# Attention by packed tokens and a gated feed-forward layer on one core: the beginning in one traced order, first softmaxes from PSUM by token halves, first batch in steps of four f tiles, Softplus/Erf gates in 32 units

## The chip, the core and the metric

The kernel runs on one core of a Trainium2 chip. Its engines are TensorE (PE; its weight loads are PEld), VectorE (DVE), ScalarE (ACT), GpSimd (POOL) and SyncE (SP), which issues most DMAs. Each runs its own instructions in order and waits for the others by semaphores. The metric is the device time of one execution in microseconds; several executions were timed, and one more was recorded by the profiler.

## The reference, cut to what matters

```python
# 8 batches, 8 heads, 576 tokens, head_dim 64, 32 packed tokens, d_model 512, d_ff 2048
p_packed = sm_attn(p, k, v)                  # the 32 packed tokens look at k and v
out = sm_attn(q, p_packed, p_packed)         # every token looks at the packed tokens
x = out.transpose(0, 2, 1, 3).reshape(B * S, H * D)
h = x @ w_in                                 # w_in, w_out: float64 arrays
sp = np.maximum(h, 0.0) + np.log1p(np.exp(-np.abs(h)))     # softplus
g = h * erf(sp)
return (g @ w_out).astype(np.float32)
```

## The kernel before, in words

**Units.** A batch b has 576 tokens, taken in two halves c of 288. The 2048 columns of d_ff are taken in eight steps i of 256 (two f tiles of 128). A unit is one (b, c, i); there are 128. Batches 0 and 1 come in four segments each: steps 0 to 3 of both halves of batch 0, the same of batch 1, then steps 4 to 7 of batch 0, then of batch 1. The batches 2 to 7 go through all eight steps of one half before the other. Where a batch comes in two turns, the second turn adds to the output in memory by an accumulating DMA of POOL (L318); the first writes by SP (L320).

**Work of a unit.** `h_block`: 12 matmuls (L264) give h for 256 columns, as three products of split operands: `a2h` and `a2l` are the high and low part of the second softmax (transposed), `wph` and `wpl` those of wp = p_packed times w_in. ACT copies h from PSUM into `hs` (L267). The gate h * erf(softplus(h)) is approximated by four ACT functions, Tanh, Square, Tanh, Tanh (L270, L271, L272, L275), and three DVE instructions (L273, L274 and a last multiplication, L280 or L283). `o_block`, LAG = 3 units later: the unit's share of g @ w_out (L308). For the first WHOLE = 12 units g and w_out go in as F32, 16 matmuls; after that both are split into two parts (g: L286, L287; w_out: `woh` L103 on ACT, `wol` L104 on DVE), 24 matmuls. At a segment's end ACT copies the sums out (`ob`, L315).

**Attention and wp.** `attention(b)` is a generator of 12 stages, which the main loop advances between units: first scores `s` (L165), softmax over 576 tokens (L170 to L179), transposes `t` (L186), the packed tokens `p` (L198), second scores `s` (L212), softmax over the 32 packed tokens in a transposed layout (L215 to L229), `a2h`, `a2l` (L232, L233). `w_prime(b, j)` computes one of four wp blocks of 512 columns (L243; copies L245, L246). Attention of batch 1 begins with unit 0 (ATT1).

**Weights.** w_in and w_out arrive as float64, in 32 tiles of 128 x 512 (512 KB each). `load_f32` issues the DMA into a staging tile (L83), ACT takes the high words to F32 (L87), and three DVE instructions put the bits together (L88, L89, L90). The staging pool `spool` has two places; six early loads borrow places of `wpool` (EARLY). A load into a place waits until the conversion that used it before has ended. Tile names: `wi_c` is block c of w_in on its way, `wos` a tile of w_out on its way, `wo` the converted one.

**Order.** The program is traced unit by unit, with a plan that attaches stages, loads and conversions to units; a scheduler then orders each engine's instructions by its own estimate of times. Nothing else pins the order, except one `high_priority` block.

Of the kernel before, what the change touches and what calls it, by code (L numbers as in the profile page):

```python
# [28 lines left out]
def tile_pack_attention_moe(ctx: ExitStack, tc: tile.TileContext, qT, kT, v, pT, w_in, w_out, outT):  # L29
# [23 lines left out]
    CONV = 2  # L53
# [22 lines left out]
    def load_f32(dst, src, name, pool=None, tag="wst"):  # L76

        if src.dtype == F32:
            nc.sync.dma_start(dst, src)
            return  # L80
        n = src.shape[1]
        st = (pool or spool).tile([P, n], I64, name=name, tag=tag)
        nc.sync.dma_start(st[:], src)  # L83
# [3 lines left out]
        nc.scalar.activation(dst, high.bitcast(F32), AF.Abs, scale=F64_SCALE)  # L87
        nc.vector.tensor_scalar(bits, bits, 3, None, op0=ALU.logical_shift_left)  # L88
        nc.vector.scalar_tensor_tensor(bits, high, 0x80000000, bits, op0=ALU.bitwise_and, op1=ALU.bitwise_or)  # L89
        nc.vector.scalar_tensor_tensor(bits, low, 29, bits, op0=ALU.logical_shift_right, op1=ALU.bitwise_or)  # L90

    def load_w_in(j, c, **slot):
        load_f32(w_in_sb[:, c, j * FB:(j + 1) * FB], w_in[c * P:(c + 1) * P, j * FB:(j + 1) * FB], f"wi{j}_{c}", **slot)

    def load_w_out(f, **slot):
        made = opool.tile([P, DM], F32, name=f"wo{f}", tag="wo")
        load_f32(made[:], w_out[f * P:(f + 1) * P, :], f"wos{f}", **slot)
        wo[f] = made

    def split_w_out(f):  # L100
# [4 lines left out]
        wo_hi[f], wo_lo[f] = hi, lo  # L105

# [7 lines left out]
    def attention(b, roomy=False):  # L114
# [45 lines left out]
        a1 = apool.tile([P, 2, S], F32, name=f"a1_{b}", tag="big")  # L160
        for c2 in range(2):
# [8 lines left out]
        nc.vector.tensor_reduce(m[:], a1[:], axis=AX.X, op=ALU.max)  # L170
        nc.vector.tensor_scalar(m[:], m[:], -SCALE, None, op0=ALU.mult)
        sm = apool.tile([P, 2], F32, name=f"sm{b}", tag="sm")
        for r in range(2):
            nc.scalar.activation(a1[:, r, :], a1[:, r, :], AF.Exp, bias=m[:, r:r + 1], scale=SCALE,
                                 accum_out=sm[:, r:r + 1])
# [7 lines left out]
        for j in range(NT):  # L183
            for r in range(2):
                o = (j % 2 * 2 + r) * P
                nc.tensor.transpose(banks[0][j // 2][:, o:o + P], a1[:, r, j * P:(j + 1) * P], ident[:])  # L186
        copy_out(a1t[:, 0:NT].rearrange("p (x j) r k -> p x (j r k)", x=2), banks, 512)
# [5 lines left out]
        nc.scalar.copy(a1t[0:REM, NT].rearrange("p r k -> p (r k)"), pr[0:REM, 0:2 * P])  # L193
        for j in range(NCH):
# [8 lines left out]
        nc.vector.tensor_copy(ptt[:], po[:, 0:P])  # L203
        pt[b] = ptt
        yield
        nb = HT // 32
        ta = apool.tile([P, 2, S], F32, name=f"ta{b}", tag="big")
        for c2 in range(2):
# [5 lines left out]
            for r in range(2):  # L214
                nc.vector.transpose(ta[:, r, c2 * HT:(c2 + 1) * HT], banks[0][r][:, 0:HT])  # L215
            yield
        blocks = ta[:].rearrange("p r (n k) -> p (r n) k", k=NK)
        mx = apool.tile([P, 4 * nb], F32, name=f"mx{b}", tag="mx")
        wide = mx[:].unsqueeze(2).to_broadcast([P, 4 * nb, NK])
        nc.vector.tensor_reduce(mx[:], blocks, axis=AX.X, op=ALU.max)  # L220
        nc.vector.tensor_tensor(blocks, blocks, wide, op=ALU.subtract)
        nc.scalar.activation(ta[:], ta[:], AF.Exp, scale=SCALE)
        yield
        nc.vector.tensor_reduce(mx[:], blocks, axis=AX.X, op=ALU.add)
        nc.vector.tensor_scalar(mx[:], mx[:], 1e-9, None, op0=ALU.add)
        nc.vector.reciprocal(mx[:], mx[:])
        nc.vector.tensor_tensor(blocks, blocks, wide, op=ALU.mult)
        tb = apool.tile([P, 2, S], F32, name=f"tb{b}", tag="big")
        nc.vector.transpose(tb[:].rearrange("p r s -> p (r s)"), ta[:].rearrange("p r s -> p (r s)"))  # L229
        hi = apool.tile([P, 2, S], F32R, name=f"a2h{b}", tag="a2h")  # L230
        lo = apool.tile([P, 2, S], F32R, name=f"a2l{b}", tag="a2l")
        nc.scalar.copy(hi[:], tb[:])  # L232
        nc.vector.tensor_tensor(lo[:], tb[:], hi[:], op=ALU.subtract)  # L233
        a2[b] = (hi, lo)
        yield

    def w_prime(b, j):
        hi = wpool.tile([P, 2, FB], F32R, name=f"wph{b}_{j}", tag="wph")
# [7 lines left out]
        nc.vector.tensor_tensor(lo[:], ps[:], hi[:], op=ALU.subtract)  # L246
        wp[b, j] = (hi, lo)

    gs = {}

    def h_block(b, c, i, whole):


        hs = tpool.tile([P, 2, HT], F32, name=f"hs{b}_{c}_{i}", tag="hs")
        for k in range(2):
# [4 lines left out]
            n = 0  # L260
            ahi, alo = a2[b]
            for r in range(2):
                for w, a in ((whi, ahi), (whi, alo), (wlo, ahi)):
                    nc.tensor.matmul(ps[:, 0:HT], w[:, r, fo:fo + P], a[:, r, c * HT:(c + 1) * HT],  # L264
                                     start=(n == 0), stop=(n == 5))
                    n += 1
            nc.scalar.mul(hs[:, k, :], ps[:, 0:HT], 0.5)  # L267
# [8 lines left out]
        if whole:  # L276
            k = len(wholes) % 2
            wholes.append(i)
            g = tpool.tile([P, 2, HT], F32, name=f"g{b}_{c}_{i}", tag=("gh", "gl")[k], bufs=2)
            nc.vector.scalar_tensor_tensor(g[:], t[:], 1.0, hs[:], op0=ALU.add, op1=ALU.mult)  # L280
            gs[b, c, i] = (g,)
            return
        nc.vector.scalar_tensor_tensor(hs[:], t[:], 1.0, hs[:], op0=ALU.add, op1=ALU.mult)  # L283
        ghi = tpool.tile([P, 2, HT], F32R, name=f"gh{b}_{c}_{i}", tag="gh", bufs=2)
        glo = tpool.tile([P, 2, HT], F32R, name=f"gl{b}_{c}_{i}", tag="gl", bufs=2)
        nc.vector.tensor_copy(ghi[:], hs[:])  # L286
        nc.vector.tensor_tensor(glo[:], hs[:], ghi[:], op=ALU.subtract)  # L287
        gs[b, c, i] = (ghi, glo)
# [35 lines left out]
    segs = [(b, c, i0, i1) for i0, i1 in zip(TURNS, TURNS[1:]) for b in range(NB0) for c in range(2)]  # L324
# [15 lines left out]
    plan = {}  # L340
    conv = {}
    for i in range(NBLK):
        ph = max(n for n, start in enumerate(TURNS) if i >= start)
        items = []
        if i % 2 == 0:
            items += [("wi", i // 2, c) for c in range(4)]
        items += [("wo", 2 * i), ("wo", 2 * i + 1)]
        conv.setdefault(ph, []).append(items)
    for ph, lists in conv.items():
        if ph == 0:  # L350
            for k, items in enumerate(lists):
                for it in items:
                    at(WI_AT[k // 2] if it[0] == "wi" else k + 1).append(it)
        else:
            flat = [it for items in lists for it in items]
            n0, n1 = (2 * NB0 * TURNS[p] for p in (ph - 1, ph))
            for k, it in enumerate(flat):
                at(n0 + CONV + k * (n1 - n0 - 2 * CONV) // len(flat)).append(it)
# [18 lines left out]
    for k, (b, j) in enumerate(uses):  # L377
        if b not in ready:
# [8 lines left out]
    for f in range(DFF // P):  # L387
        made = max(n for n, its in plan.items() if ("wo", f) in its)
# [84 lines left out]
```

## Time and profile before

| what | value |
|---|---|
| executions timed | 793.75, 792.89, 793.60 us, median 793.6 us |
| profiled execution | 789.89 us, its span 788.1 us, mean granted clock 0.968 |
| PE busy | 744.6 us, 94% of the span |
| DVE busy, ACT busy | 599.7 us (76%), 597.6 us (76%) |
| POOL busy | 15.1 us (2%) |
| read from memory, written | 45.61 MB, 11.80 MB |

The profiled execution is 3.7 us shorter than the median of the timed ones; times of single pieces are from it. In the lines of the profile, L12 is line 12 of the kernel printed above, `out<-in` names the tiles that are written and read, `xN` counts instructions, and a bracket at a line's end gives the engine's idle time ahead of it and what ended it.

### The profile page before, as it was taken

To read this page: it belongs to the slowest core of one execution; us is meant where nothing else is said; L and a number is where in the kernel's file an instruction comes from. 1 tells how busy PE (TensorE), PEld (TensorE's weight loads), DVE (VectorE), ACT (ScalarE), POOL (GpSimd) and SP (SyncE) were. 2 spreads that over 40 slices of the span, in tenths; PEclk is the share of its full clock that TensorE was granted. 3 is DMA by queue.
4 is the path that set the end of the run, shared out by engine and by line. 5 is a ranking of instruction groups with operands and counts; after the bars stand their busy time and mean duration, and the time that the engine had idled before them with its cause. 6 is when DMAs were issued, how large, how long until landed. Compare 5 with 4: busy or idle time off the path is not lost.

```text
span 788.1 us, 15219 instructions
## 1 busy us (share of the span) xinstructions
PE 744.6 (94%) x6256; PEld 664.1 (84%) x6256; DVE 599.7 (76%) x916; ACT 597.6 (76%) x1011; POOL 15.1 (2%) x22
## 2 busy tenths in 40 slices
PE   3549988999999999999999999999999999999998
PEld 2228756899998898899799998889888998899998
DVE  3887898977689678867887769767886769766664
ACT  3357778988689878887687868778687867878784
POOL 0000000000111100000000000000000000000000
PEclk8568999999999999999999999999999999999999
DMA  8834735002542422013200222002300210000000
GB/s 306 291 110 149 243 116 162 31 17 67 107 88 31 83 76 89 1 39 98 80 32 1 83 81 72 13 1 80 132 32 1 79 47 1 31 2 31 1 31 31
DMA packets 31813, 58.39 MB, mean 74 GB/s; under 512 B 3584, under 2 KB 14848, under 8 KB 31744
## 3 DMA queue, kind: packets, MB, share of 16 engines
q1 hardware_dynamic: 29440, 55.06, 21.5%
q0 software_dynamic: 2304, 2.36, 2.6%
q8 instruction: 49, 0.80, 0.4%
q14 instruction: 20, 0.16, 0.1%
HBM read 45.61 MB, written 11.80 MB: 73 GB/s over the span
## 4 chain that ended last, share of the span: by engine, by line
PE 82%; DVE 7%; DMA 6%; ACT 3%; issue 1%; SPq 0%; ACTq 0%
PE o L308 50%; PE h L264 24%; PE wp L243 4%; DMA wi<-w_in 4%; DMA wos<-w_out 2%; PE p L198 2%; PE s L212 1%; PE s L165 1%; PE t L186 1%; DVE w_in_sb L89 1%; ACT t L270 1%; DVE wo L89 1%; ACT wo L87 1%; DVE w_in_sb L90 1%; DVE g L280 0%
## 5 line engine op out<-in xcount | busy, mean ns | idle before, releaser
L308 PE MATMUL o<-gl,woh 128*128 128x288 f32 x928 | 273.3, 295 | 0.0
L308 PE MATMUL o<-gh,woh 128*128 128x288 f32 x928 | 273.1, 300 | 0.0
L308 PE MATMUL o<-gh,wol 128*128 128x288 f32 x928 | 272.9, 295 | 0.0
L308 PEld LDWEIGHTS o<-gh,woh 128*128 128x128 f32 x928 | 172.1, 187 | 25.5 <-DVE t L273 8.9
L308 PEld LDWEIGHTS o<-gl,woh 128*128 128x128 f32 x928 | 174.3, 188 | 1.8 <-issue 1.3
L308 PEld LDWEIGHTS o<-gh,wol 128*128 128x128 f32 x928 | 174.6, 188 | 1.5 <-issue 1.3
L267 ACT ACTIVATE hs<-h 128x288 f32<-128x288 f32 x256 | 103.2, 412 | 95.4 <-PE h L264 94.6
L264 PE MATMUL h<-a2h,wph 128*128 128x288 f32 x512 | 155.2, 304 | 10.6 <-ACT wph L245 5.9
L264 PE MATMUL h<-a2l,wph 128*128 128x288 f32 x512 | 152.7, 298 | 1.8 <-DVE a2l L233 1.8
L264 PE MATMUL h<-a2h,wpl 128*128 128x288 f32 x512 | 152.6, 298 | 0.0
L283 DVE SCALAR_TENSOR_TENSOR hs<-t,hs 128x576 f32<-128x576 f32 x116 | 87.7, 756 | 72.5 <-ACT t L275 72.5
L275 ACT ACTIVATE t<-t,bias 128x576 f32<-128x576 f32 x128 | 98.8, 772 | 25.3 <-DVE t L274 25.0
L264 PEld LDWEIGHTS h<-a2h,wph 128*128 128x128 f32 x512 | 97.2, 190 | 22.3 <-ACT wph L245 6.8
L273 DVE SCALAR_TENSOR_TENSOR t<-t,hs 128x576 f32<-128x576 f32 x128 | 95.9, 750 | 20.1 <-ACT u L272 19.8
L270 ACT ACTIVATE t<-hs,bias 128x576 f32<-128x576 f32 x128 | 99.6, 778 | 2.9
L271 ACT ACTIVATE t<-t,bias 128x576 f32<-128x576 f32 x128 | 99.3, 775 | 2.3
L264 PEld LDWEIGHTS h<-a2l,wph 128*128 128x128 f32 x512 | 97.4, 190 | 4.3 <-DVE a2l L233 2.8
L272 ACT ACTIVATE u<-t,bias 128x576 f32<-128x576 f32 x128 | 99.3, 776 | 1.8
L264 PEld LDWEIGHTS h<-a2h,wpl 128*128 128x128 f32 x512 | 97.3, 190 | 1.9 <-issue 1.9
L274 DVE SCALAR_TENSOR_TENSOR t<-u,t 128x576 f32<-128x576 f32 x128 | 96.3, 752 | 1.6
L287 DVE TENSOR_TENSOR gl<-hs,gh 128x576 fp32r<-128x576 f32 x116 | 87.3, 753 | 1.5
L286 DVE CAST gh<-hs 128x576 fp32r<-128x576 f32 x116 | 52.9, 456 | 35.0 <-PE o L308 33.8
(60 smaller groups left out, 637.3 us busy)
## 6 DMA issues: line engine op xcount, KB each, us to landing
k<-kT SPq DMA_DIRECT2D x32, 288.0 KB, 4.3
q<-qT SPq DMA_DIRECT2D x32, 288.0 KB, 4.3
outT<-ob SPq DMA_DIRECT2D x64, 144.0 KB, 1.8
wi<-w_in SPq DMA_DIRECT2D x16, 512.0 KB, 6.0
v<-v SPq DMA_DIRECT2D x32, 256.0 KB, 3.6
wos<-w_out SPq DMA_DIRECT2D x16, 512.0 KB, 3.6
outT<-ob POOLq DMA_DIRECT2D x16, 144.0 KB, 3.7
v<-v SPq DMA_DIRECT2D x8, 128.0 KB, 4.2
```

The source lines that it names most:

```text
L264: nc.tensor.matmul(ps[:, 0:HT], w[:, r, fo:fo + P], a[:, r, c * HT:(c + 1) * HT], start=(n == 0), stop=(n == 5))
L267: nc.scalar.mul(hs[:, k, :], ps[:, 0:HT], 0.5)
L270: nc.scalar.activation(t[:], hs[:], AF.Tanh, bias=bias[:, 0:1], scale=2.0 * T_SCALE)
L271: nc.scalar.activation(t[:], t[:], AF.Square, bias=bias[:, 1:2], scale=Q_SCALE)
L272: nc.scalar.activation(u[:], t[:], AF.Tanh, bias=bias[:, 2:3], scale=U_SCALE)
L273: nc.vector.scalar_tensor_tensor(t[:], t[:], 0.5 * A2, hs[:], op0=ALU.mult, op1=ALU.add)
L274: nc.vector.scalar_tensor_tensor(t[:], u[:], 0.5 * A1, t[:], op0=ALU.mult, op1=ALU.add)
L275: nc.scalar.activation(t[:], t[:], AF.Tanh, bias=bias[:, 3:4], scale=2.0 * A_SCALE)
L283: nc.vector.scalar_tensor_tensor(hs[:], t[:], 1.0, hs[:], op0=ALU.add, op1=ALU.mult)
L286: nc.vector.tensor_copy(ghi[:], hs[:])
L287: nc.vector.tensor_tensor(glo[:], hs[:], ghi[:], op=ALU.subtract)
L308: nc.tensor.matmul(acc[b, c][d][:, 0:HT], w[f][:, d * P:(d + 1) * P], gg[:, k, :], start=(first and k == 0 and n == 0), stop=(last and k = ...
```

## The change

- **Gates.** In the first 32 units (GROUPED) the gate is Softplus, Erf (ACT) and one multiplication (DVE). The gates come in 13 groups (ENDS gives the last unit of each): all Softplus of a group, then all Erf, each kind behind an `ACT_TABLE_LOAD`; `in_turn` fixes the order of these functions on ACT. In these units o blocks follow five units behind (LAG_G) and not three, and `hs` alternates between two tags by groups. From unit 32 on the gate is the one of before.
- **Segments.** Batch 0's steps 0 to 3 come as two turns (0 to 1 and 2 to 3, each for both halves), so there are ten segments in batches 0 and 1, with eight more output tiles of 128 x 288 copied by ACT and added by POOL than before.
- **Whole units.** WHOLE goes from 12 to 8. w_out is split from unit 7 on (SPLIT) and not from 14.
- **Beginning.** The first stages, loads, conversions and two units are written out by hand, and `keep_order` ties each instruction of PE, DVE, ACT and SP there to the one before it in the traced order. 33 dummy matmuls (`keep_busy`: 6, 10, 3, 14) on the identity stand among them.
- **First attention.** For batch 0 (`roomy`) the scores stay in PSUM: maxima and exponentials read them there, by halves of 288 tokens, and the second softmax goes by two halves (`Tokens`, near and far).
- **Plan.** Attention of batch 1 is attached to units 1 to 5, not 0 to 2; the conversions are attached by FIRST and LATER. The cast of a conversion is a multiplication by 2^-112, not Abs with that scale.

```diff
@@ constants @@
+    GROUPED = 4 * NBLK
+    LAG_G = 5
...
-    TURNS = (0, NBLK // 2, NBLK)
-    WHOLE = 12
-    SPLIT = 14
-    WI_AT = (-1, 1)
-    ATT1 = (0, 2)
+    HB = NBLK // 2
+    WHOLE = 2 * HB
+    SPLIT = 7
+    ATT1 = (1, 5)
...
+    FIRST = {0: [("wo", 2), ("wo", 3)], 1: [("wi", 1, c) for c in range(4)],
+             3: [("wo", 4), ("wo", 5)], 4: [("wo", 6), ("wo", 7)]}
+    LATER = (5, 14)
+    ENDS = (1, 3, 5, 7, 10, 13, 15, 18, 21, 24, 27, 29, 31)
@@ attention @@
-            copy_out(a1[:, :, c2 * HT:(c2 + 1) * HT], banks, HT)
+            if roomy:
+                scores.append(banks[0])
+            else:
+                copy_out(a1[:, :, c2 * HT:(c2 + 1) * HT], banks, HT)
...
+        near, far = Tokens(0, HT), Tokens(HT, S)
+        for c2, half in enumerate((near, far)):
+            for r in range(2):
+                nc.vector.transpose(ta[:, r, half.cols], scores[2 + c2][r][:, 0:HT])
+            if half is near:
+                near.max()
+                near.exp()
+        yield
+        near.sum()
+        near.turn()
+        near.high()
...
@@ gates @@
+    def gate_group():
+
+        ts = []
+        for hs, b, c, i, whole in group:
+            t = tpool.tile([P, 2, HT], F32, name=f"t{b}_{c}_{i}", tag="t0")
+            in_turn(nc.scalar.activation(t[:], hs[:], AF.Softplus))
+            ts.append(t)
+        for t in ts:
+            in_turn(nc.scalar.activation(t[:], t[:], AF.Erf))
+        for t, (hs, b, c, i, whole) in zip(ts, group):
+            if whole:
+                nc.vector.tensor_tensor(whole_g(b, c, i)[:], t[:], hs[:], op=ALU.mult)
+            else:
+                nc.vector.tensor_tensor(hs[:], t[:], hs[:], op=ALU.mult)
+                split_g(hs, b, c, i)
+        group.clear()
@@ segments @@
-    segs = [(b, c, i0, i1) for i0, i1 in zip(TURNS, TURNS[1:]) for b in range(NB0) for c in range(2)]
+    turns = [(0, 0, HB // 2), (0, HB // 2, HB), (1, 0, HB), (0, HB, NBLK), (1, HB, NBLK)]
+    segs = [(b, c, i0, i1) for b, i0, i1 in turns for c in range(2)]
@@ beginning @@
+    def keep_busy(n):
+
+        for _ in range(n):
+            nc.tensor.matmul(idle[:, 0:P], ident[:], ident[:], start=True, stop=True)
+
+    start = len(traced)
     first = attention(0, roomy=True)
...
+    (b4, e4), (b5, e5) = fetch("wo", 0), fetch("wo", 1)
+    keep_busy(6)
...
+    h_block(*units[1][:3], True, 1)
+    end = len(traced)
...
+        while behind <= n - (LAG_G if n < GROUPED else LAG):
+            o_block(*units[behind])
+            behind += 1
+    keep_order(start, end)
```

In the rows of the order the batch number is left out of a name: in `o_1_0_3`, `h_0_0_0` or `hs_0_1` the first digit is the half c, the second the step i, a third the column tile; the last number is a running one.

First, ACT ahead of the first gates of batch 1 (`t_0_0` is the gate of its first unit). Before:

```order
L270 ACTIVATE t_0_0_936<-hs_0_0_919,bias 128x576
L271 ACTIVATE t_0_0_936<-t_0_0_936,bias 128x576
L272 ACTIVATE u_0_0_937<-t_0_0_936,bias 128x576
L87 ACTIVATE wo_1100<-wos_1101 128x512
L267 ACTIVATE hs_0_1_966<-h_0_1_0_967 128x288
L267 ACTIVATE hs_0_1_966<-h_0_1_1_975 128x288
L245 CAST wph_3_1040<-wp_3_1042 128x1024
L270 ACTIVATE t_0_1_983<-hs_0_1_966,bias 128x576
L267 ACTIVATE hs_0_2_1007<-h_0_2_0_1008 128x288
L275 ACTIVATE t_0_0_936<-t_0_0_936,bias 128x576
```

After, ahead of the same unit's Erf, in the group of its first three units:

```order
L404 COPY hs_0_1_969<-h_0_1_0_970 128x288
L115 CAST woh_1187<-wo_1176 128x512
L404 COPY hs_0_1_969<-h_0_1_1_978 128x288
L94 ACTIVATE wo_1252<-wos_1253 128x512
L404 COPY hs_0_2_1012<-h_0_2_0_1013 128x288
L374 ACTIVATE t_0_1_1031<-hs_0_1_969 128x576
L404 COPY hs_0_2_1012<-h_0_2_1_1021 128x288
L374 ACTIVATE t_0_2_1033<-hs_0_2_1012 128x576
L377 ACT_TABLE_LOAD
L377 ACTIVATE t_0_0_1029<-t_0_0_1029 128x576
L377 ACTIVATE t_0_1_1031<-t_0_1_1031 128x576
L377 ACTIVATE t_0_2_1033<-t_0_2_1033 128x576
```

Before, four functions of a unit stand by themselves, with a weight cast now and then between two of them; after, three units' functions stand behind the last cast of a weight tile (`wos_1253` is the 32nd load).

Second, PE around batch 1's first unit (`h_0_0_0`; `wp` are its wp blocks and the later ones of batch 0). Before:

```order
L308 MATMUL o_1_0_3_910<-g_1_2_836,wo_661 128x288
L243 MATMUL wp_2_784<-w_in_sb,pt_237 32x512 x8
L308 MATMUL o_1_0_0_907<-g_1_3_894,wo_713 128x288
L308 MATMUL o_1_0_0_907<-g_1_3_894,wo_720 128x288
L308 MATMUL o_1_0_1_908<-g_1_3_894,wo_713 128x288
L308 MATMUL o_1_0_1_908<-g_1_3_894,wo_720 128x288
L308 MATMUL o_1_0_2_909<-g_1_3_894,wo_713 128x288
L308 MATMUL o_1_0_2_909<-g_1_3_894,wo_720 128x288
L308 MATMUL o_1_0_3_910<-g_1_3_894,wo_713 128x288
L308 MATMUL o_1_0_3_910<-g_1_3_894,wo_720 128x288
L264 MATMUL h_0_0_0_920<-a2h_597,wph_0_601 128x288
L264 MATMUL h_0_0_1_928<-a2h_597,wph_0_601 128x288
```

After, from the instruction behind batch 0's last o block of the first turns on:

```order
L255 MATMUL s_0_1_627<-q_1_471,pt_624 32x288 x2
L255 MATMUL s_0_1_627<-q_1_472,pt_624 32x288 x2
L255 MATMUL s_0_1_627<-q_1_473,pt_624 32x288 x2
L255 MATMUL s_0_1_627<-q_1_474,pt_624 32x288 x2
L255 MATMUL s_1_1_669<-q_1_471,pt_624 32x288 x2
L255 MATMUL s_1_1_669<-q_1_472,pt_624 32x288 x2
L255 MATMUL s_1_1_669<-q_1_473,pt_624 32x288 x2
L255 MATMUL s_1_1_669<-q_1_474,pt_624 32x288 x2
L346 MATMUL wp_0_735<-w_in_sb,pt_624 32x512 x8
L346 MATMUL wp_1_748<-w_in_sb,pt_624 32x512 x8
L346 MATMUL wp_2_802<-w_in_sb,pt_269 32x512 x8
L400 MATMUL h_0_0_0_903<-a2h_681,wph_0_733 128x288
```

Before, a wp block stands between two o blocks of batch 0, and the second scores stand further ahead; after, batch 1's second scores and the wp blocks follow the last o block and precede the first h.

Third, DVE where the first block of the second quarter of w_in is finished (`wi_0`; its last instruction frees a staging place). Before:

```order
L88 TENSOR_SCALAR wo_572<-wo_572 128x512
L89 SCALAR_TENSOR_TENSOR wo_410<-wos_411,wo_410 128x512
L88 TENSOR_SCALAR w_in_sb<-w_in_sb 128x512
L89 SCALAR_TENSOR_TENSOR wo_565<-wos_566,wo_565 128x512
L88 TENSOR_SCALAR w_in_sb<-w_in_sb 128x512
L89 SCALAR_TENSOR_TENSOR wo_572<-wos_573,wo_572 128x512
L233 TENSOR_TENSOR a2l_274<-tb_271,a2h_273 128x1152
L90 SCALAR_TENSOR_TENSOR wo_410<-wos_411,wo_410 128x512
L89 SCALAR_TENSOR_TENSOR w_in_sb<-wi_0_417,w_in_sb 128x512
```

After:

```order
L380 TENSOR_TENSOR g_0_1_398<-t_0_1_392,hs_0_1_373 128x576
L97 TENSOR_SCALAR wo_400<-wo_400 128x512
L97 TENSOR_SCALAR wo_407<-wo_407 128x512
L98 SCALAR_TENSOR_TENSOR wo_400<-wos_401,wo_400 128x512
L97 TENSOR_SCALAR w_in_sb<-w_in_sb 128x512
L98 SCALAR_TENSOR_TENSOR wo_407<-wos_408,wo_407 128x512
L97 TENSOR_SCALAR w_in_sb<-w_in_sb 128x512
L99 SCALAR_TENSOR_TENSOR wo_400<-wos_401,wo_400 128x512
L98 SCALAR_TENSOR_TENSOR w_in_sb<-wi_0_414,w_in_sb 128x512
L99 SCALAR_TENSOR_TENSOR wo_407<-wos_408,wo_407 128x512
L98 SCALAR_TENSOR_TENSOR w_in_sb<-wi_1_420,w_in_sb 128x512
L99 SCALAR_TENSOR_TENSOR w_in_sb<-wi_0_414,w_in_sb 128x512
```

After, the multiplications of the first gate group stand ahead of it (the first row is the second of them), and four conversions go in turns; before, the low part of batch 0's softmax stands among four conversions.

More of the change, by code (lines that the diff above doesn't have):

```diff
@@ L221, in attention @@
[L221 to L227, printed above, removed]
+            if roomy:
+                scores.append(banks[0])
+            else:
+                for r in range(2):
+                    nc.vector.transpose(ta[:, r, c2 * HT:(c2 + 1) * HT], banks[0][r][:, 0:HT])
+                yield
@@ L235, in attention @@
+        yield
+        near.sum()
+        near.turn()
+        near.high()
+        yield
+        far.max()
+        near.low()
+        yield
+        far.exp()
+        yield
+        far.sum()
+        far.turn()
+        far.high()
+        yield
+        far.low()
         yield
```

282 lines of the change are left out of this document (192 added, 90 removed).

## The prediction

> **What bounds the kernel now.** I read the page first: busy time, slices, chain.
>
> ```profile
> span 788.1 us, 15219 instructions
> PE 744.6 (94%) x6256; PEld 664.1 (84%) x6256; DVE 599.7 (76%) x916; ACT 597.6 (76%) x1011; POOL 15.1 (2%) x22
> PE   3549988999999999999999999999999999999998
> PEclk8568999999999999999999999999999999999999
> PE 82%; DVE 7%; DMA 6%; ACT 3%; issue 1%; SPq 0%; ACTq 0%
> ```
>
> PE is the bound, except at the left end: a slice is 19.7 us, and the seven first slices hold all the gaps (but the end's) and all the reduced clock. The windows (length, then busy time of PE, PEld, DVE, ACT, POOL with instruction counts, granted clock, DMA share, GB/s) put edges on that:
>
> ```profile
> 0.00:64.00 64.00, 29.79 (x259) 18.83 (x260) 44.00 (x80) 28.69 (x48) 0.70 (x6) 0.65 0.67 229
> 64.00:140.00 76.00, 69.83 (x471) 51.09 (x470) 64.80 (x102) 58.53 (x101) 0.00 (x0) 0.96 0.51 164
> 140.00:236.00 96.00, 96.00 (x786) 88.71 (x785) 76.13 (x119) 80.73 (x145) 7.28 (x8) 1.00 0.27 63
> ```
>
> From 140 us on PE never stops. So the end of the kernel is: the time at which PE has its work without gaps, plus the PE work then left. Everything in the change is worth what it does to these two. The pieces and counts of PE (timeline and chain: start, length; groups up to 138.1 us: count, busy, mean ns) say where before stands at that time:
>
> ```profile
> 42.53 0.85 PE L264 MATMUL h<-a2h,wph 128*128 128x288 f32 x2 [4.24 <-ACT a2h L232]
> 131.84 4.04 PE L308 MATMUL o<-g,wo 128*128 128x288 f32 x16
> 138.10 6.09 PE o L308 x24
> 144.19 1.60 PE h L264 x12
> 172.72 3.19 PE o L308 x24
> L308 PE MATMUL o<-g,wo 128*128 128x288 f32 x145 | 39.6, 429 | 1.8 <-DVE g L280 1.8
> L264 PE MATMUL h<-a2h,wph 128*128 128x288 f32 x52 | 18.1, 354 | 10.6 <-ACT wph L245 5.9 <-ACT a2h L232 4.2 <-ACT hs L267 0.5
> ```
>
> An h block is 1.60 us (12 records, 4 of each kind), a split o block 3.19 (24 records), a whole one 4.04 (16). Up to 138.1 PE has done 52/4 = 13 h blocks and 145/16 = 9 whole o blocks; then the gapless part starts, with batch 1's second unit (the first ran alone at 131.84).
>
> What holds it back until then is the weights. They come as 64-bit words through two staging places, cast on ACT (L87), finished by three DVE instructions (L88 to L90); a new load waits on SP until a conversion has freed a place. SP's own loads and waits:
>
> ```profile
> 48.15 1.83 SPq L83 DMA_DIRECT2D wi<-w_in  x2
> 118.96 0.34 SPq L83 DMA_DIRECT2D wi<-w_in  x1
> 120.69 12.62 SPq L83 DMA_DIRECT2D wos<-w_out  x4
> L83 SPq DMA_DIRECT2D wos<-w_out x12: 327/328/340, 57.3 to 133.0; - x12
> L83 SPq DMA_DIRECT2D wi<-w_in x8: 327/328/632, 48.1 to 119.0; - x8
> DMA to landing us min/median/max: 3.4/3.8/6.0
> SPq L83 <- DVE wo L90: 31.3, 12, 7.9
> SPq L83 <- DVE w_in_sb L90: 30.7, 9, 7.2
> 48.15:133.00 84.85, 72.01 (x487) 52.69 (x487) 70.96 (x114) 62.89 (x107) 0.00 (x0) 0.91 0.52 167
> ```
>
> 20 of the 32 loads are such refills, from 48.15 to 133.0: 19 steps of 4.47 us. SP spends 31.3 + 30.7 us of them waiting for L90. DVE is busy in 84% of the stretch (70.96 of 84.85), so a conversion often queues there behind gates and attention. The durations that I use:
>
> ```profile
> L87 ACT ACTIVATE wo<-wos 128x512 f32<-128x512 f32 x16 | 10.6, 672 | 6.0 <-DMA wos<-w_out 6.0
> L88 DVE TENSOR_SCALAR wo<-wo 128x512 uint32<-128x512 uint32 x11 | 4.6, 422 | 2.8 <-ACT wo L87 2.7
> L89 DVE SCALAR_TENSOR_TENSOR wo<-wos,wo 128x512 uint32<-128x512 uint32 x13 | 8.9, 685 | 0.1
> L90 DVE SCALAR_TENSOR_TENSOR wo<-wos,wo 128x512 uint32<-128x512 uint32 x14 | 9.6, 684 | 0.0
> L267 ACT ACTIVATE hs<-h 128x288 f32<-128x288 f32 x256 | 103.2, 412 | 95.4 <-PE h L264 94.6
> L270 ACT ACTIVATE t<-hs,bias 128x576 f32<-128x576 f32 x128 | 99.6, 778 | 2.9
> L275 ACT ACTIVATE t<-t,bias 128x576 f32<-128x576 f32 x128 | 98.8, 772 | 25.3 <-DVE t L274 25.0
> L273 DVE SCALAR_TENSOR_TENSOR t<-t,hs 128x576 f32<-128x576 f32 x128 | 95.9, 750 | 20.1 <-ACT u L272 19.8
> L286 DVE CAST gh<-hs 128x576 fp32r<-128x576 f32 x116 | 52.9, 456 | 35.0 <-PE o L308 33.8
> L287 DVE TENSOR_TENSOR gl<-hs,gh 128x576 fp32r<-128x576 f32 x116 | 87.3, 753 | 1.5
> L104 DVE TENSOR_TENSOR wol<-wo,woh 128x512 fp32r<-128x512 f32 x6 | 4.1, 684 | 0.0
> L315 ACT COPY ob<-o 128x288 f32<-128x288 f32 x80 | 30.2, 399 | 6.8 <-PE o L308 6.8
> L71 ACT ACT_TABLE_LOAD x1 | 1.3, 1283 | 0.7 <-PEq L465 0.7
> ```
>
> **The change, part by part.**
>
> *Gates of the first 32 units.* Four ACT functions become two: 32 x 2 x 0.778 = 49.8 us less. The order has 35 table loads against 1: 34 x 1.283 = 43.6 us more. ACT is 6 us better off. DVE loses two instructions a unit: 32 x 2 x 0.75 = 48 us less. Behind 140 us none of it counts, PE being full; before, it frees DVE for conversions. Softplus and Erf are not in this trace; I take them at L270's 0.778 (same shape). At half of it ACT would gain 25 us more over 32 units, at twice it would lose 50; neither end is near, since the four functions of before lie within 6 ns of each other. The one table load of the trace took 1.283 us, on an idle ACT. The Trainium skill (ScalarE: Activation LUTs, section What ACT_TABLE_LOAD costs) puts some 1380 ns of drain on top of those 1283 for every switch to another set; by it ACT would come out 41 us worse off, not 6 better, and the sum would be about 810 instead of 800. The load agrees, the drain no row here shows.
>
> *Beginning and first softmax.* Scores are read from PSUM and the softmax goes by halves of 288 tokens, most conversions behind it. In before its passes run from 28 to 42.5 us, of this size (timeline, first and last of eight):
>
> ```profile
> 30.56 1.35 DVE L220 TENSOR_REDUCE mx<-ta 128x36 f32<-128x1152 f32 x1
> 41.33 1.15 ACT L232 CAST a2h<-tb 128x1152 fp32r<-128x1152 f32 x1 [1.42 <-DVE tb L229]
> ```
>
> Halved, and without the conversions that stand among them, they let the first h begin by my estimate at 28 to 31 us instead of 42.5. Two h blocks at half clock (6.4), two copies not hidden (0.8), two table loads (2.6) and four functions (3.1) then put the first gates' end at about 42, and batch 0's first four units need nothing but weights that are already there. This lead is real, and it is off the path: what PE does early is work that PE would otherwise have done while waiting later. The 33 dummy matmuls stand where PE waits; they cost nothing while PE has gaps there, and 33 x 0.13 (3.19/24) = 4 us, 9 at half clock, if it had none.
>
> *Refills.* This term decides. The order shows ten loads issued freely and 22 refills, against 20 before, and on DVE the first place comes free only behind the first group's two multiplications and, interleaved with three others, the ninth conversion: 42 + 0.8 + 12 x 0.6 = about 49.4. That is before's 48.15 again: the early start does not start the refills. From there 21 steps. Bounds for a step: a bare round is landing 3.8, cast 0.67, three instructions 1.79, with two places 3.1 us; the slow end is before's 4.47. For the value I scale by DVE: before has 114 instructions in this stretch, after by its order 103 (20 conversions, 13 wo splits, four wpl, batch 1's softmax, six gates of one multiplication), so 84.85 x 103/114 = 76.7 us. ACT in the same stretch gets nine table loads (11.5) and eight more output copies (3.2) and drops 12 functions of those six gates (9.3): +5.4, of which I count half, 2.7, since half of ACT's waits here lie beside a landing. Last refill: 49.4 + 76.7 + 2.7 = 128.8, a step of 3.78.
>
> *Order in front of batch 1.* In before batch 1's first gate stands behind the cast of the 29th weight tile. In after the cast of the 32nd, the last, stands on ACT ahead of the first Softplus's companions and of all Erfs of the group. So 128.8 is followed by landing 3.8, cast 0.67, two copies 0.82, two Softplus 1.56, table load 1.28, first Erf 0.78, and on DVE three multiplications, one wol, gh and gl in their order, 4.6: PE goes on at 142.3. PE cannot fill that time: its order has, between batch 0's last o and batch 1's first h, only batch 1's second scores and three wp.
>
> *Work left behind that point.* After has done 12 h blocks and 8 whole o blocks. It has 1.60 of h more to do; 4 x 3.19 of split o where before had 3 x 4.04 of whole o: 1.60 + 12.76 - 12.12 = +2.2 us. (Eight whole o blocks instead of twelve are a gain of 4 x 0.85 over the run, contained in this.)
>
> *Small things at nothing:* eight more accumulating output DMAs on POOL (busy 2%), the cast by a multiplication instead of Abs (same engine and shape), copies without the factor 0.5. Their cover is ACT's gaps; bare they are below 1 us.
>
> Sum: 142.3 - 138.1 + 2.2 = +6.4. The profiled execution took 789.9 us, so 796.3; the median of the runs shown, 793.6, lies 3.7 above it, so **800.0**. PE goes gapless at X: the result is 793.6 + X - 135.9.
>
> Clock: it was granted at 0.65 up to 64 us, with PE busy less than half of the time; the hole between batch 0's last o (about 98) and batch 1's first h can bring that back. Three h blocks and three wp at half clock cost up to 6 us more of PE, and nothing at the other end, since PE waits there for the gate; I take nothing.
>
> **The rivals.**
>
> *The round gets short (faster).* If casts and conversions always find ACT and DVE free, a step falls toward 3.1; at 3.2 the last refill goes at 116.6, X is 130.1, the result 787.8. For it: 48 us fewer DVE gate instructions, SP waiting 62 us for L90 before. Against: in after's order 13 wo splits and batch 1's softmax stand among the last ten conversions. It decides below a step of 3.48 (X = 135.9).
>
> *Nothing moves.* DVE's scaling alone without ACT's 2.7, and a tail shorter by 2: X = 137.6, the result 795.3; with refills from 47 it is 793. The start at 48 to 49 in both kernels speaks for it.
>
> *Table loads cost more than their row (slower).* If a load among gates must first let ACT run empty and so holds it twice as long, the nine in the refill stretch cost 11.5 more, half counted 5.8. Behind X, ACT has 24 gates of the new kind at 0.82 + 1.56, 22 loads and 16 output copies, 92 us; 28 more make 120, against PE's 24 x 3.19 + 20 x 1.60 + batch 2's attention of about 9 = 118, with ACT's waits for PE on top, some 4 more: 810. For it: ACT has no other long row that alternates its functions. Against it: ACT is idle for a quarter of the time, and a drain would partly lie there. The page named above has this case as its rule.
>
> **How the numbers follow.** Forecast (X 138 to 157, 796 to 815): 0.42. Shorter round: 0.30. Nothing moves: 0.14. Dear table loads (800 to 815, beside the forecast's own spread): 0.14. A measurement of this kernel tells 0.2%, 1.6 us, from no change. Faster is the short round, plus a little of nothing-moves: 0.32. Same: 0.13. Slower: 0.55. The low end is a step of 3.1 with a tail 2 us shorter, X = 126, 783; the high end before's own 4.47: last refill 143.3, X = 156.8, 814.5. Less than 2 in 10 lie outside. The likeliest case alone has 796 to 812.
>
> **What would show it.** First h near 30, first o near 43: the beginning is right. Refills from about 49 to 129 in 21 steps: the deciding term. PE idle between about 98 and 130 with the release by wo, w_in_sb or wph: the hole. ACT's cast of the last wo tile waiting for its DMA just ahead of the first group of three Erfs: the tail. Wrong I am if refills start well before 45 (a place freed early), if the step is under 3.5, if PE still has gaps behind 145 with ACT full (table loads), or if the DVE instructions overlap more than now.

## The result, and the profile after

The changed kernel takes 805.99 us in the median of four runs (805.10 to 808.86) where the kernel before takes 793.67 (792.89 to 794.35): a ratio of 1.0162, with a 95% interval of 1.0134 to 1.0189. It is slower, as forecast, but by 12.3 us and not by 6.4. The profiled execution is the longest of the four, 808.86 us; its page, to be held against the lines shown of before:

```profile
span 806.9 us, 15383 instructions
PE 751.1 (93%) x6354; PEld 670.8 (83%) x6354; DVE 565.8 (70%) x874; ACT 593.2 (74%) x993; POOL 22.7 (3%) x30
PE   7687853799999999999999999999999999999998
PEclk9879965899999999999999999999999999999999
PE 77%; ACT 8%; DMA 7%; DVE 5%; issue 2%; SPq 0%; ACTq 0%
```

The first slices of PE are fuller than before (7687 against 3549), and a new hole stands in the sixth and seventh (5 and 3), with the clock down. The windows (columns as before) put a size on it:

```profile
0.00:64.00 64.00, 48.55 (x347) 34.78 (x348) 39.09 (x78) 30.02 (x55) 0.70 (x6) 0.84 0.59 200
64.00:140.00 76.00, 45.35 (x335) 27.75 (x334) 54.86 (x89) 47.09 (x77) 7.42 (x8) 0.77 0.64 186
140.00:236.00 96.00, 90.06 (x752) 81.86 (x753) 45.96 (x75) 70.02 (x119) 3.54 (x4) 0.97 0.22 60
```

Ahead of 64 us PE is busy for 18.8 us more than before (11.6 of it the dummies), then for 24.5 less up to 140 and 5.9 less behind. What the early start gives is given back, and more. The hole's edges on PE (timeline: start, length, and in brackets the idle time ahead and what ended it):

```profile
44.56 7.20 PE L444 MATMUL o<-g,wo 128*128 128x288 f32 x16 [3.31 <-DVE g L380]
125.49 1.96 PE L346 MATMUL wp<-w_in_sb,pt 64*32 64x512 f32 x16 [6.78 <-DVE wpl L350]
137.86 0.85 PE L400 MATMUL h<-a2h,wph 128*128 128x288 f32 x2 [3.88 <-ACT a2h L298]
156.21 0.80 PE L444 MATMUL o<-gh,woh 128*128 128x288 f32 x4 [1.29 <-DVE gh L358]
158.91 0.40 PE L400 MATMUL h<-a2h,wph 128*128 128x288 f32 x1 [0.32 <-ACT hs L404]
```

What PE waits for between 100 and 140 us (in total, times, longest):

```profile
PE wp L346 <- DVE wpl L350: 11.3, 2, 6.8
PE h L400 <- ACT a2h L298: 3.9, 1, 3.9
PE s L255 <- DVE pt L246: 2.6, 1, 2.6
PE wp L346 <- DVE ta L261: 2.5, 1, 2.5
PE h L400 <- DVE a2l L301: 1.0, 1, 1.0
PE s L255 <- DVE ta L261: 1.0, 1, 1.0
```

These 22.3 us are all waits for steps of batch 1's attention and for wp blocks; none is for a converted weight or a gate.

SP's first and last refills, the landing times of the refills, and the window between the two:

```profile
50.82 0.94 SPq L88 DMA_DIRECT2D wi<-w_in  x2
132.62 11.81 SPq L88 DMA_DIRECT2D wos<-w_out  x4
DMA to landing us min/median/max: 3.4/4.3/6.0
50.82:144.10 93.28, 62.63 (x425) 39.53 (x424) 64.19 (x103) 55.89 (x95) 7.42 (x8) 0.80 0.62 183
```

The last of SP's four loads from 132.62 on goes at 144.1. From 158.9 on PE is gapless but for 1.8 us. Two things come late ahead of it. The refills: from 50.8 to 144.1, 21 steps of 4.44 us, as slow as before's 4.47 although DVE is now busy for 69% of the stretch only (64.19 of 93.28) and not 84%. And batch 1's attention: its `a2h`, without which no h of batch 1 begins, is cast at 136.7 us, in before at 114.6 (timeline of ACT, before's row first):

```profile
114.58 1.15 ACT L232 CAST a2h<-tb 128x1152 fp32r<-128x1152 f32 x1
136.67 1.14 ACT L298 CAST a2h<-tb 128x1152 fp32r<-128x1152 f32 x1
```

The two are not apart: the steps of batch 1's softmax stand on DVE between conversions. Ahead of the transpose whose result `a2h` is cast from, 27 of the 32 conversions are finished, 17 of them refills; in before it is 25 and 13. Four more refills at 4.44 us and a first refill 2.7 us later make 20.4 of the 22.1 us by which `a2h` comes later, an estimate from these counts.

### The profile page after: what moved, and what is told of

The parts are those of the page before. It is cut to its first block, busy times and chain, and to the rows that moved or that the text cites. A ratio compares the mean times of both kernels' runs of the same rounds, so it can differ in the third digit from the quotient of the medians.

```text
span 806.9 us, 15383 instructions
## 1 busy us (share of the span) xinstructions
PE 751.1 (93%) x6354; PEld 670.8 (83%) x6354; DVE 565.8 (70%) x874; ACT 593.2 (74%) x993; POOL 22.7 (3%) x30
## 4 chain that ended last, share of the span: by engine, by line
PE 77%; ACT 8%; DMA 7%; DVE 5%; issue 2%; SPq 0%; ACTq 0%
PE o L444 47%; PE h L400 22%; DMA wos<-w_out 3%; PE wp L346 3%; DMA q<-qT 2%; PE p L241 2%; DMA wi<-w_in 1%; PE s L255 1%; ACT L374 1%; ACT t L374 1%; DMA v<-v 1%; PE s L188 1%; ACT hs L404 1%; ACT L377 1%; ACT t L377 1%
## 5 line engine op out<-in xcount | busy, mean ns | idle before, releaser
L444 PE MATMUL o<-gh,woh 128*128 128x288 f32 x960 | 283.4, 300 | 1.4 <-DVE gh L358 1.3
L444 PE MATMUL o<-gl,woh 128*128 128x288 f32 x960 | 283.1, 296 | 0.0
L444 PE MATMUL o<-gh,wol 128*128 128x288 f32 x960 | 282.5, 295 | 0.0
L406 ACT ACTIVATE hs<-h 128x288 f32<-128x288 f32 x192 | 77.9, 413 | 75.8 <-PE h L400 73.1
L423 DVE SCALAR_TENSOR_TENSOR hs<-t,hs 128x576 f32<-128x576 f32 x96 | 72.6, 757 | 56.3 <-ACT t L419 56.2
L419 ACT ACTIVATE t<-t,bias 128x576 f32<-128x576 f32 x96 | 74.2, 773 | 19.3 <-DVE t L418 18.8
L417 DVE SCALAR_TENSOR_TENSOR t<-t,hs 128x576 f32<-128x576 f32 x96 | 71.9, 749 | 15.3 <-ACT u L416 15.3
L414 ACT ACTIVATE t<-hs,bias 128x576 f32<-128x576 f32 x96 | 74.6, 777 | 2.3
L416 ACT ACTIVATE u<-t,bias 128x576 f32<-128x576 f32 x96 | 74.7, 778 | 1.8
L415 ACT ACTIVATE t<-t,bias 128x576 f32<-128x576 f32 x96 | 74.1, 772 | 1.5
L418 DVE SCALAR_TENSOR_TENSOR t<-u,t 128x576 f32<-128x576 f32 x96 | 72.3, 753 | 0.8
```

The source lines that it names most:

```text
L414: nc.scalar.activation(t[:], hs[:], AF.Tanh, bias=bias[:, 0:1], scale=2.0 * T_SCALE)
L415: nc.scalar.activation(t[:], t[:], AF.Square, bias=bias[:, 1:2], scale=Q_SCALE)
L416: nc.scalar.activation(u[:], t[:], AF.Tanh, bias=bias[:, 2:3], scale=U_SCALE)
L417: nc.vector.scalar_tensor_tensor(t[:], t[:], 0.5 * A2, hs[:], op0=ALU.mult, op1=ALU.add)
L418: nc.vector.scalar_tensor_tensor(t[:], u[:], 0.5 * A1, t[:], op0=ALU.mult, op1=ALU.add)
L419: nc.scalar.activation(t[:], t[:], AF.Tanh, bias=bias[:, 3:4], scale=2.0 * A_SCALE)
```

## The experiments

All times are against runs of the kernel before on the same chip in the same session, so ratios are compared; before's median lay between 791.0 and 792.2 us in these sessions. "Changed" is the changed kernel at 1.0162. The bands of the expectations are meant beside 793.6 us for the kernel before, unless they name another time. An edit changes the scheduler's order behind it too; where that matters, the trace is read.

### Is it the staging round?

e1, a third place for the changed kernel, and e2, the same edit for the kernel before:

```diff
-    spool = ctx.enter_context(tc.tile_pool(name="stage", bufs=2))
+    spool = ctx.enter_context(tc.tile_pool(name="stage", bufs=3))
```

> The changed kernel with three staging places in place of two, nothing else (the scheduler orders anew). Theory A (the time is set by the round trip of a staging place: landing, wait for ACT, cast, wait for DVE, three instructions, 8.9 us a place, so 4.44 us a refill with two): with three a refill takes about 3 us, DVE's 64 us of work in the stretch then bound it, the last load goes near 120 instead of 144, PE is gapless from about 132 instead of 156, the kernel takes about 782. Theory B (the round is not it: batch 1's softmax and wp blocks on DVE, the table loads and PE's order in front of batch 1 set the end): loads come earlier, but the kernel stays above 800.

> The kernel before with three staging places. Theory A: the same bound stood there, 4.47 us a refill; with three places DVE's 71 us bound the stretch from 48, so the last load goes near 120 instead of 133 and the kernel takes about 782. Theory B: within 3 us of 793.6.

Measured: e1 1.0089 (1.0071 to 1.0108), 799.9 us; e2 1.0026 (1.0015 to 1.0038), 793.7 us. SP's last load and ACT's a2h, of e1 and then of e2:

```profile
116.90 0.33 SPq L88 DMA_DIRECT2D wos<-w_out  x1
130.47 1.15 ACT L298 CAST a2h<-tb 128x1152 fp32r<-128x1152 f32 x1 [1.91 <-DVE tb L292]
```

```profile
104.35 8.97 SPq L83 DMA_DIRECT2D wos<-w_out  x3
120.71 1.15 ACT L232 CAST a2h<-tb 128x1152 fp32r<-128x1152 f32 x1 [0.33 <-DVE tb L229]
```

The last load comes 27 us earlier in e1 and 20 us in e2. In e1 the kernel gains 0.7%, some 6 us, which is what a2h moves by; in e2 a2h comes 6 us later, and nothing is gained. By the traces more conversions are finished on DVE ahead of the transpose that feeds a2h, 31 of 32 instead of 27 in e1 and 30 instead of 25 in e2: earlier loads put more work in front of it. Theory A, that the round by itself sets the time, has fallen (it gave 782 for both kernels); it was also the prediction's deciding term. The round is worth 0.7% in the changed kernel.

### Is it the gates, the splits, the segments?

e3 sets `GROUPED = 0` (the old gates everywhere, and with them o blocks three units behind and no groups), e4 has `WHOLE = 12` and `SPLIT = 14`:

> The changed kernel with the four-function gates of before in all units (so no table loads among gates, three DVE instructions a gate, o blocks three units behind); beginning, segments and whole units stay as changed. Theory A: gates are not on the path that sets the end, the refill step stays at 4.3 to 4.6 us, 801 to 810. Theory C (table loads and grouping are the cost): 790 to 797. Theory D (lighter gates gave something back): above 812.

> The changed kernel with 12 whole units and the w_out splits from unit 14 on, as before. Theory A with the order: 14 to 16 splits leave the stretch ahead of batch 1's first gate (about 10 us on DVE, 9 on ACT), and the last weight cast stands behind the first group's Erf; PE is gapless 8 to 12 us earlier, 3.4 us more matmul time, so 797 to 802. Theory B' (splits lie in waits anyway): 807 to 811.

Measured: e3 1.0224 (1.0206 to 1.0241), some 811 us beside 793.6, between the bands of theories A and D and against theory C: with all else changed, the new gates with their grouping gain some 0.6%. e4 1.0127 (1.0112 to 1.0142): a third of a per cent back, short of theory A's gain; a2h stands at 130.2 there.

e7 has `LATER = (5, 20)`; e8 has batch 0's steps 0 to 3 in one turn for each half:

> The changed kernel with its last sixteen loads and conversions attached to units 5 to 20, not 5 to 14. In its order 31 casts instead of 32 stand ahead of batch 1's first Erf and 28 instead of 29 ahead of its a2h. Theory A or E: one refill step earlier, 3 to 6 us, 800 to 803. Otherwise unchanged, 804 to 808.

> The changed kernel with batch 0's steps 0 to 3 in one turn for each half, as before (eight output copies and eight accumulating output DMAs fewer). Theory E or A: the copies of ACT that wait for o blocks stand in front of some casts, but the refill round mostly waits for landings; 0 to 4 us less, 802 to 806. If the early output tiles and their DMAs hold up the refills (landing 4.3 us in the median instead of 3.8): 796 to 800.

Measured: e7 1.0132 (1.0110 to 1.0154), 0.3% less, somewhat under what was expected of one refill step, and its interval overlaps the changed kernel's; e8 1.0210 (1.0181 to 1.0239), missed: the finer turns gain about 0.5%, and eight more output tiles are no cost.

### Is it the place of batch 1's attention?

e5 takes back one number of the change, e6 adds the third place, e9 puts the changed number into the kernel before:

```diff
e5, e6
-    ATT1 = (1, 5)
+    ATT1 = (0, 2)
e9
-    ATT1 = (0, 2)
+    ATT1 = (1, 5)
```

> The changed kernel with batch 1's attention attached to units 0 to 2, as before, not 1 to 5. In its order batch 1's second scores and wp blocks stand among batch 0's o blocks again, and 28 of the 32 weight casts, not all 32, stand on ACT ahead of the first Erf of batch 1. Theory E (two chains of like length end in batch 1's first gate, the refills and batch 1's attention; the change delayed the second and put it behind the first): PE is gapless 14 to 20 us earlier, 787 to 795. Theory A (refills alone, by their step): the four refills that no longer stand ahead are worth the same 14 to 18 us, but with three places on top nothing more. Theory F (the attention only takes DVE's time from the conversions wherever it stands): 802 to 809.

> The changed kernel with batch 1's attention at units 0 to 2 and three staging places. Theory E: each of the two edits alone leaves the other chain, both together shorten the beginning more than the sum of their gains suggests or at least by as much: 774 to 784. Theory A: as with early attention alone. Theory F: as with three places alone, about 8 us over the kernel before.

> The kernel before with one part of the change alone: batch 1's attention attached to units 1 to 5 instead of 0 to 2. Theory E (this delay is what made the changed kernel slower): 6 to 14 us over before, 798 to 806. Theory G (the delay hurts only together with the new beginning and segments): within 3 us of before.

Measured: e5 1.0028 (1.0013 to 1.0044), 794.6 us, at the weak end of theory E's band; e6 0.9994 (0.9974 to 1.0014), 791.8 us, some 8 us above its band; e9 1.0224 (1.0192 to 1.0256), 809.5 us, more than expected. Casts of a2h in e5, e6 and e9, with SP's last loads in e5 and e9:

```profile
136.62 15.80 SPq L88 DMA_DIRECT2D wos<-w_out  x4
122.44 1.15 ACT L298 CAST a2h<-tb 128x1152 fp32r<-128x1152 f32 x1
```

```profile
119.96 1.15 ACT L298 CAST a2h<-tb 128x1152 fp32r<-128x1152 f32 x1 [1.60 <-DVE tb L292]
```

```profile
125.11 0.33 SPq L83 DMA_DIRECT2D wos<-w_out  x1
133.11 1.15 ACT L232 CAST a2h<-tb 128x1152 fp32r<-128x1152 f32 x1 [1.06 <-DVE tb L229]
```

The place of batch 1's attention is the cause of most of the loss, shown in both directions: in the changed kernel the number gives 1.3% of the 1.6% back, and alone in the kernel before it costs 2.2%. The refills cannot be behind it, since they move the other way: e5 is faster although its last load goes at 152.1 us, 8 later than in the changed kernel, and e9 is slower although its last load goes at 125.1, 8 earlier than in before.

Theory E's two separate chains are not borne out. Two chains that end together would let both edits gain more than the sum of their single gains; early attention (1.3%) and the third place (0.7%) together give 1.7%, and with the attention in its old place the third place is worth some 0.3%. What fits instead is the count above: 14 refills' conversions are finished ahead of the transpose in e5 and 19 in e9, where the changed kernel has 17 and before 13.

e10 and e11 add 12 whole units and late splits to e5 and e6:

> The changed kernel with batch 1's attention at units 0 to 2 and with 12 whole units, splits from unit 14. In its order 4 w_out splits instead of some 14 stand ahead of batch 1's first gate, and 29 of the 32 casts. Theory H (after the attention, DVE's work in the stretch from 100 to 120 us is what keeps PE waiting, and the splits are 10 us of it): 785 to 790, under the kernel before. If the refill round alone is left: 793 to 797, since the splits lie in its waits and the whole blocks cost 3.4.

> The same with three staging places. Theory H with theory E: refills and DVE are both relieved, 779 to 786. If one of the two was the whole of it: as with the better one of them, 785 to 792.

Measured: e10 1.0059 (1.0043 to 1.0076), e11 1.0018 (1.0002 to 1.0035), each 0.2 to 0.3% over its partner, below the bare price of four whole blocks (3.4 us, 0.43%). Theory H has fallen, and e11 lies above both of its bands: with the attention early, the splits lie mostly in waits. In e10 a2h is at 112.2, and the kernel gains nothing by it.

### Is earlier better?

> The changed kernel with batch 1's attention attached to units 0 to 1. In its order 20 of 32 weight casts and no w_out split stand on ACT ahead of batch 1's a2h, 22 and 4 ahead of its first Erf; with units 0 to 2 it was 25 and 11, and 28 and 12. Theory E (position of the attention among the conversions): a2h comes near 105 instead of 122 us, batch 1's units start with some ten refills still to come; PE is gapless 10 to 20 us earlier than with units 0 to 2: 772 to 784 (at 791 for the kernel before). Theory A (refill round alone): the loads that batch 0's second half needs bound instead, 788 to 795.

> The kernel before with batch 1's attention attached to units 0 to 1 instead of 0 to 2. In its order 22 or 23 instead of 27 casts stand ahead of batch 1's a2h. Theory E: a2h moves up from 118 us, 784 to 790 at 791 for the kernel before. If its slower beginning (first h at 42.5, first o at 64.8 us) bounds instead: 790 to 796.

> The changed kernel with batch 1's attention at units 0 to 1 and three staging places. If refills are the next bound: 3 to 8 us under the same with two places. If they are covered by batch 1's units by then: within 2 us of it.

> The changed kernel with all stages of batch 1's attention attached to unit 0. Its order differs little from units 0 to 1 (20 casts ahead of a2h, 24 and 6 splits ahead of the first Erf). Theory E: as with units 0 to 1 or up to 4 us slower, since batch 0's own units come later on DVE.

Edits: `ATT1 = (0, 1)` in e13 to e15 (e14 in the kernel before, e15 with three places), `(0, 0)` in e16. Measured: e13 1.0131 (1.0090 to 1.0172), e14 1.0222 (1.0190 to 1.0253), e15 1.0026 (1.0011 to 1.0040), e16 1.0142 (1.0116 to 1.0167). Except for e16's remark that it would be like e13, all of it was missed. The a2h of e13, what PE waits for from 40 to 190 us, and ACT ahead of the longest of these waits' end; then a2h and two waits of e14:

```profile
95.97 1.15 ACT L298 CAST a2h<-tb 128x1152 fp32r<-128x1152 f32 x1 [1.49 <-DVE tb L292]
PE h L400 <- ACT hs L404: 6.5, 4, 3.1
PE h L400 <- ACT wph L348: 6.1, 1, 6.1
85.85 1.16 ACT L282 ACTIVATE ta<-ta 128x1152 f32<-128x1152 f32 x1 [1.76 <-DVE ta L281]
86.92 0.99 ACT L348 CAST wph<-wp 128x1024 fp32r<-128x1024 f32 x1
```

```profile
102.81 1.13 ACT L232 CAST a2h<-tb 128x1152 fp32r<-128x1152 f32 x1
60.52 2.10 PE L186 MATMUL t<-ident,a 128*128 128x128 f32 x8 [6.94 <-DVE a L179]
77.75 1.17 PE L212 MATMUL s<-q,pt 64*32 64x288 f32 x4 [3.97 <-DVE pt L203]
```

The attention comes 12 to 41 us earlier than in the kernels it is held against, but PE, which goes in order, now waits between 60 and 100 us with batch 0's blocks queued behind. In e14 it waits for steps of batch 1's attention itself. In e13 the longest wait is for a wph cast of batch 0, which stands on ACT behind the exponentials of batch 1's second softmax; the last refill of e13 still goes at 143. PE's idle time by stretches of the traced executions (the length of a window less PE's busy time), us:

| run | ratio | a2h at | last refill | idle 0 to 100 | 100 to 140 | 140 to 236 |
|---|---|---|---|---|---|---|
| before | 1 | 114.6 | 133.0 | 34.3 | 6.1 | 0.0 |
| e9, before with late attention | 1.0224 | 133.1 | 125.1 | 36.5 | 19.1 | 2.5 |
| e14, before with earlier attention | 1.0222 | 102.8 | 130.7 | 48.5 | 4.3 | 0.0 |
| changed | 1.0162 | 136.7 | 144.1 | 23.6 | 22.5 | 5.9 |
| e5, changed with attention as before | 1.0028 | 122.4 | 152.1 | 22.9 | 16.5 | 0.7 |
| e13, changed with earlier attention | 1.0131 | 96.0 | 143.2 | 32.2 | 3.8 | 4.5 |

(The traced execution of e13, 797.7 us, lies 6 us under its median.) So of the places tried units 0 to 2 are the best, in both kernels: later, batch 1 is held up behind 100 us; earlier, batch 0 is held up ahead of it. The third place is worth 1% in e15 against e13, more than expected: there refills did come next.

### Table loads, the dummies, and one version more

e12 has `ENDS = tuple(range(4 * NBLK))`, one group for each unit; e18 has no dummy matmuls; e17 is e6 with `LATER = (5, 20)`:

> The changed kernel with a group for each of the 32 units, so about 38 more table loads, each on ACT between two functions. At the row's price, 1.283 each, that is 49 us more of ACT, a third of it ahead of batch 1's first gate; ACT's gaps there and 17 us of spare time behind take most: 808 to 820. With a drain of 1.38 on top of each (Theory C): 101 us more, ACT then is the bound behind 156 us, 835 to 860.

> The changed kernel without its 33 dummy matmuls. If the gaps of PE cover them and they only keep the clock up while nothing on PE decides: 804 to 808, as with them. If the clock they keep carries the early lead into the rest: 809 to 816. If they stood in the way: below 803.

> The changed kernel with batch 1's attention at units 0 to 2, three staging places, and the last sixteen conversions attached to units 5 to 20. If conversions on DVE ahead of batch 1's softmax are what is left: 783 to 788 at 791.5 for the kernel before. If not (the order still has 29 casts ahead of a2h): 789 to 794.

Measured: e12 1.0484 (1.0452 to 1.0516), 25.5 us more than the changed kernel for 35 more loads (70 against 35). Both kernels' loads as groups, with mean and the idle time ahead, first of the changed kernel:

```profile
L374 ACT ACT_TABLE_LOAD x15 | 19.2, 1283 | 0.3
39.16 1.28 ACT L374 ACT_TABLE_LOAD   x1
40.46 1.26 ACT L374 ACTIVATE t<-hs 128x576 f32<-128x576 f32 x2
```

```profile
L374 ACT ACT_TABLE_LOAD x32 | 41.1, 1283 | 0.6
140.00:236.00 96.00, 80.45 (x584) 70.12 (x585) 46.17 (x71) 89.75 (x128) 0.00 (x0) 0.91 0.14 44
```

A load takes 1283 ns at each place. But for one or two loads in each trace, a load starts within 0.02 us of the end of the function ahead, and the next function within 0.02 us of the load's end. 35 loads are 44.9 us of ACT, of which 25.5 show: ACT is busy 89.75 of 96 us from 140 to 236 and PE waits. The time lies between the two bands of the expectation, so it does not decide by itself; the rows leave no room for the further 1.38 us on a load.

e18 1.0246 (1.0223 to 1.0269): without the dummies 0.8% slower, the second case of its expectation. Where the time goes I cannot show: up to 140 us the two traces have PE busy alike but for the first 20 us, where most dummies are; from 140 to 200 it is 52.97 against 55.44 us. The traced executions lie 2.8 us apart and the medians 5.6 (of two sessions), since the traced one of the changed kernel is 2.9 above its median.

e17 0.9946 (0.9926 to 0.9965), 787.8 us at 792.2 for before: faster than both kernels, in the first band of its expectation. a2h, the last refills and a window:

```profile
116.09 1.14 ACT L298 CAST a2h<-tb 128x1152 fp32r<-128x1152 f32 x1
111.07 9.65 SPq L88 DMA_DIRECT2D wos<-w_out  x4
140.00:200.00 60.00, 59.91 (x487) 57.23 (x487) 26.29 (x42) 46.52 (x77) 0.00 (x0) 1.00 0.12 38
```

PE is full from 140 us on, with three settings of the changed kernel changed. Held against e6, the later conversions are worth 0.5%, in e7 0.3%. Why is not shown: in e6 as in e17, 27 conversions are finished ahead of the transpose that feeds a2h.

## Why the prediction was right and wrong

Right: the direction, and that the early start does not last. The first h was forecast for 28 to 31 us and came at 32.7, the first o at 43 and came at 44.6; the first refill goes at 50.8 (forecast 49.4, where the terms that it names add up to 50.0), so the start of the refills did not move with the start of the work. DVE has the 103 instructions of the forecast in the stretch, busy 64 us. The new gates are no cost (e3), and the whole units are a small term (e4, e10).

Wrong, as a mechanism: the working gave no price to batch 1's attention. It saw the second scores and wp blocks move behind batch 0's last o block, and called the hole a wait for refills, which these could not fill. Its own sign for that was PE idle with the release by `wo`, `w_in_sb` or `wph`; the 22.3 us of waits between 100 and 140 us end with `wpl`, `a2h`, `pt`, `ta` and `a2l` instead. e1 shows that with the refills out of the way by 117 us more than half of the loss stays. e5 and e9 show that the move of the attention is worth 1.3% one way and 2.2% the other, while the last refill moves against the time. What fits these runs is the number of refills' conversions ahead of the attention's steps, each worth about a step, and not how early the last refill goes.

Wrong, as a term of the sum: the refill step. It was put at 3.78 us by scaling with DVE's instruction count and measured 4.44, which makes 13.9 of the 16.6 us by which the gapless point came later (158.9 for 142.3; the start gave 1.4, the tail 14.8 for 13.5). The scaling was the mistake. A step is half of a place's round: 8.9 us in both kernels, of which landing, cast and three instructions are 6.3 in before and 6.8 in the changed kernel by their medians and means, the rest waiting. With DVE less busy the waiting shrank by about half a microsecond, and the landings grew by as much, from 3.8 to 4.3 us in the median.

The forecast's number is nearer than its parts, and that is luck. With 158.9 for X its formula gives 816.6 us, and 806.0 were measured. Of the 10.6 us between, 6.6 are the choice of the profiled executions (2.9 above the median after, 3.7 below it before), and 2.1 are work: by 158.9 PE had done 13 h blocks and four matmuls of a split o block, where the forecast had 12 h blocks. The other 1.9 are not accounted for.

The rivals: the short round with a faster kernel did not come (with two places the step was 4.0 to 4.8 us in all runs), nor did dear table loads: no run shows the drain that the Trainium skill adds (ScalarE: Activation LUTs, What ACT_TABLE_LOAD costs); its 1283 ns are what every load took. The dummies, put at nothing while PE has gaps, are worth 0.8% (e18), so that term was wrong too, in the kernel's favour. And in the hole the clock was low (0.61 granted from 100 to 140 us): wp blocks there take 1.96 us and not 1.09, which was put at nothing.

The parts of the change, so far as single edits tell: gates 0.6% to the good (e3), finer turns 0.5% (e8), dummies 0.8% (e18); whole units and splits 0.35% to the bad (e4), the later attention 1.3% (e5). They do not simply add, since each edit is ordered anew: added up they would make the changed kernel a little faster than before, and it is 1.6% slower. The beginning in its fixed order, the first softmax by halves and the places of the early loads (FIRST) were not taken back by any run, so what they cost or gain stays open.

## What to carry to other kernels

When a stretch of work moves in the order of a pipeline, even by one number, price what will stand ahead of it on each engine that goes in order. Here batch 1's softmax stood on DVE behind conversions that waited for their loads, and each refill more ahead of it cost 3 to 5 us, about a step. The place had an optimum among those tried, with 1 to 2% lost on both sides of it. A faster supply alone gained 0.7% or nothing, as it put more conversions ahead of the same steps. In this ring of two buffers a step was half a round, and a lighter engine took only some of the waiting out of it. And a gap in PE is best read by what ends it before it is given a cause.

## What the runs showed of the hardware

An `ACT_TABLE_LOAD` held ACT for 1283 ns and nothing visible beyond, with 35 of them in the changed kernel as with 70 in e12. The landing of a 512 KB load of weights took 3.4 to 6.0 us, and its median moved from 3.8 us before to 4.3 in the changed kernel; with a third place it was 5.0 (e1):

```profile
DMA to landing us min/median/max: 3.5/5.0/6.6
```

The same shows in the other pairs (e2 4.2 for 3.8, e6 4.5 for 4.3, e15 5.5 for 4.4): here a deeper ring paid part of its gain back in slower landings.
